# First head pair of a clustered attention: tokens paired in a transpose, loads of 1536 bytes, one head's chain at a time

## The chip, the core and the metric

One core of a Trainium2 chip runs the whole program. TensorE (PE) does matmuls and transposes, and PEld is its weight load; VectorE is DVE, ScalarE is ACT, GpSimd is POOL, and SP (SyncE) issues most transfers. The metric is the time of one execution on the device, in microseconds. The median of three runs of the kernel before is 1048.67 us (1047.87 to 1049.45).

## The reference, cut to what matters

Attention in which a query sees only the keys of its own cluster comes first; two mixtures of experts follow, and the change does not touch them.

```python
B, H, S, D = 2, 8, 768, 64          # 16 clusters per head
q_n, k_n, c_n = (x / (norm(x) + 1e-6) for x in (q, k, centroids))
q_assign = argmax(einsum('bhsd,hcd->bhsc', q_n, c_n), -1)
k_assign = argmax(einsum('bhsd,hcd->bhsc', k_n, c_n), -1)
mask   = q_assign[..., :, None] == k_assign[..., None, :]
scores = where(mask, q @ k.T / sqrt(D), -1e9)
attn   = softmax(scores)
x      = attn @ v                    # then two expert mixtures
```

## The kernel before, in words

Two heads make a pair and there are eight pairs. An item is one tile of 128 queries of one head against its 768 keys, so a pair has 12 items, and the attention 96 (`attention`, L618). Each fp32 operand is split into a rounded part `hi` and a remainder `lo`, and products are taken as hi·hi + lo·hi + hi·lo.

For an item PE makes the scores `S` (`scores`, L490: two matmuls of 128 rows, two of 80; L504), DVE takes their maximum `nm` (L507), ACT the exponential `P` (`expo`, L510), PE turns `P` round in six transposes (`ptrans`, L518), ACT copies the result out as `ph` (L527) and DVE makes the remainder `pl` (L528). From item 4 on PE also multiplies by the values (`pv`, L530). The scores run two items ahead (AHEAD = 2). The first step of the loop therefore makes the scores of item 2, and it takes the PSUM buffer that item 0's exponential must have read: there are two `S` buffers.

Before its scores a pair needs a preparation (`prep`, L197). Its q and k are loaded with 128 tokens on the partitions and both heads' 64 dimensions side by side, so each token gives a run of 256 bytes for a head. `turn` (L278) transposes three tiles of 128x128, `copies` (L289) makes `hi` on ACT, `low` (L302) makes `lo`. `sims` (L318) multiplies by the normalised centroids, `product` (L340) turns that back to tokens, and the steps `a0` to `a6` of `arg_first` (L382) take the argmax on DVE and write it as one-hot rows 64 to 79 of the operands `L2` and `R2`. For the first pair this is done head by head, `a00` to `a60` for the first and `a01` to `a51` and `onehot` for the second; a same-cluster score is shifted up by a large number through these 16 rows, which is the mask. `rows0` and `rows1` (L439) copy `hi` and `lo` by SBUF transfers of 192 KB into `L1, L2, R1, R2` of the two heads.

To begin before these transfers land, items 0 and 1 take the three products straight from `hi` and `lo` with 64 rows (`products`, L479, steps `O 0` and `O 1`; six matmuls each, L486), and only the 16 mask rows are added later (`S 0`, `S 1`, two matmuls each). `E 0` and `E 1` are their exponentials.

The order is written by hand. `START` lists the steps ahead of the loop; each step issues its instructions on every engine's queue in that order, and every engine runs its queue in order. `W 24` is 24 matmuls of no use, which keep PE running while the loads are on their way. The steps with a `1` in front prepare the second pair. `FIRST` places the rest in the loop by (item, position): position 0 is behind the item's scores, 1 ahead of its transposes, 2 at its end. SP's queue has the transfers in the same order. PSUM tiles of tag `T` go round three buffers; tag `PV` has one, used by the transposes `k0`, `k1`, `q0` of the second pair (L281) as well as by `pv`. In the second pair `copies` makes two ACT copies of each transpose, and POOL subtracts them (L306).

Of the kernel before, what the change touches and what calls it, by code (L numbers as in the profile page):

```python
# [5 lines left out]
F32 = mybir.dt.float32  # L6
F32R = mybir.dt.float32r
# [21 lines left out]
def r2(ap):  # L29
    return ap.rearrange("p (a b) -> p a b", a=2)  # L30

# [51 lines left out]
class Net:  # L83
# [13 lines left out]
    def consts(self):  # L97
# [9 lines left out]
        self.cb = c.tile([128, 4, 160], F32R, name="cb")  # L107
        nc.gpsimd.memset(self.cb.bitcast(F32), 0.0)
# [26 lines left out]
    def centroids(self, p):  # L135
# [4 lines left out]
        xx = p.tile([128, 2 * D], F32, name="cxx", bufs=1)  # L140

        def scale():
            r = self.cr
            nc.vector.tensor_scalar(r, r, 1e-6, None, op0=ALU.add)
            nc.vector.reciprocal(r, r)
            nc.vector.tensor_scalar(xx[:, 0:D], x, r, None, op0=ALU.mult)
            nc.vector.tensor_scalar(xx[:, D:2 * D], x, r, None, op0=ALU.mult)

        def place():
            ps = self.ps.tile([128, 128], F32, name="cT", tag="T", bufs=3)  # L150
            nc.tensor.transpose(ps, xx, self.ident)
            ch = p.tile([128, 128], F32R, name="ch")
            cl = p.tile([128, 128], F32R, name="cl")
            nc.scalar.activation(ch, ps, AF.Copy)
            nc.vector.tensor_tensor(cl, ps, ch.bitcast(F32), op=ALU.subtract)
            for hh in range(2):
                rows = slice(hh * 64, hh * 64 + 64)
                for part, src in ((0, ch), (1, cl)):
                    sv = src[rows].bitcast(F32).rearrange("p (a h c) -> p a h c", a=4, h=2)[:, :, hh, :]
                    o = 32 + part * 64 + hh * 16  # L160
                    nc.gpsimd.tensor_copy(self.cb[rows, :, o:o + 16], sv)
# [9 lines left out]
        return norm, scale, place  # L171
# [25 lines left out]
    def prep(self, n):  # L197
# [4 lines left out]
        first = n == 0  # L202
# [12 lines left out]
        def square(s, m, hh=None):  # L215
            def go():
# [4 lines left out]
                if hh is not None:  # L221
                    nc.scalar.activation(P["sq"][:, s, :, hh], x[m][:, :, hh * 64:hh * 64 + 64], AF.Square)
                    return
# [6 lines left out]

        def total(s, hh):
            nc.vector.tensor_reduce(P["sqs"][:, s, :, hh], P["sq"][:, s, :, hh], axis=AX.X, op=ALU.add)

        def power(s, hh):
            o = self.rn2[0][:, hh * 2 * NT:hh * 2 * NT + 2 * NT, 0].rearrange("p (t s) -> p t s", s=2)
            nc.gpsimd.tensor_tensor(o[:, :, s], P["sqs"][:, s][:, :, hh], self.half[:, 0:NT], op=ALU.pow)
# [14 lines left out]
        def vsplit(hh):  # L251
            def go():

                if hh == 0:
                    P["vv"] = self.vvp.tile([128, NT, 4, 64], F32R, name="vv", tag="vv")
                hi, lo = P["vv"][:, :, 3 * hh, :], P["vv"][:, :, 1 + hh, :]
                xv = x["v"][:, :, hh * 64:hh * 64 + 64]
                if ON["vhi"] == "act":
                    nc.scalar.activation(hi, xv, AF.Copy)
                else:  # L260
                    nc.vector.tensor_copy(hi, xv)
                nc.gpsimd.tensor_tensor(lo, xv, hi.bitcast(F32), op=ALU.subtract)
            return go

        scales = {"q": 0.125, "k": 1.0}
# [74 lines left out]
        def product():  # L340
            sn = P["sn"] = self.ps.tile([128, NT, 64], F32, name="sn", tag="T", bufs=3)
# [3 lines left out]
        def arg1():  # L345
            product()
            sn = P["sn"]
# [992 lines left out]
```

## Time and profile before

| | us |
|---|---|
| median of three runs | 1048.67 |
| the profiled execution, its own time | 1048.17 |
| its span in the profile | 1046.1 |
| TensorE's mean granted clock (share of full) | 0.997 |

The profiled execution lies 0.5 us below the median, and its span 2.07 us below its own time, which is what lies around the span. Starts are us from the start of the span. In a timeline row come start, duration, engine, line, operation, out<-in, shapes, count, and in brackets the idle time ahead and what ended it. Merged rows cover several instructions.

### The profile page before, as it was taken

What the parts mean: (1) busy time and instruction counts of PE and PEld (TensorE: products, weight loads), DVE (VectorE), ACT (ScalarE), POOL (GpSimd) and SP (SyncE); (2) the same over time, 40 slices, a digit from 0 to 9 for tenths busy, and PEclk for the clock granted to TensorE, in tenths of its full rate; (3) what the DMA queues carried; (4) which work ended last, traced back from release to release, by engine and by line L of the source; (5) the groups of instructions that cost most, each with busy time, mean ns of one, the idle gap of its engine ahead of it and who ended that gap; (6) DMA issues with size and microseconds to landing.
All of it is one profiled execution on the core that took longest, in us unless ns stands there. A gap on an engine that the chain in (4) does not pass through costs nothing.

```text
span 1046.1 us, 16203 instructions
## 1 busy us (share of the span) xinstructions
PE 1031.5 (99%) x5795; PEld 962.8 (92%) x5795; DVE 812.5 (78%) x1414; ACT 544.0 (52%) x1150; POOL 631.1 (60%) x577
## 2 busy tenths in 40 slices
PE   8999999999999999999999999999999999999998
PEld 6999999998999999999999899899889989989987
DVE  7899999998887777777787876776777876676675
ACT  5989989889654444444354333333353333333320
POOL 6676677988676868666768444444444644444430
PEclk8999999999999999999999999999999999999999
DMA  9668977663122222122212221221213221221201
GB/s 197 154 153 191 207 163 179 141 161 101 51 69 72 61 81 61 62 61 65 78 40 81 81 81 41 81 81 41 81 61 122 81 81 46 76 81 59 63 21 60
DMA packets 86543, 95.94 MB, mean 92 GB/s; under 512 B 42752, under 2 KB 59488, under 8 KB 86464
## 3 DMA queue, kind: packets, MB, share of 16 engines
q1 hardware_dynamic: 86320, 94.89, 33.5%
q8 instruction: 45, 0.74, 0.3%
q14 instruction: 34, 0.28, 0.1%
q10 hardware_dynamic: 144, 0.03, 0.0%
HBM read 65.07 MB, written 3.19 MB: 65 GB/s over the span
## 4 chain that ended last, share of the span: by engine, by line
PE 84%; DVE 5%; POOL 4%; ACT 3%; DMA 2%; issue 2%; SPq 0%; DVEq 0%; POOLq 0%; ACTq 0%
PE ph L886 34%; PE po L1207 8%; PE po L1208 8%; PE po L1206 8%; PE po L985 7%; PE S L504 5%; PE T L524 4%; PE PV L537 2%; PE PV L538 2%; DMA L<-loq 1%; PE T L286 1%; PE sn L343 1%; PE sT L325 1%; DVE ph L921 1%; DVE pl L528 1%
## 5 line engine op out<-in xcount | busy, mean ns | idle before, releaser
L1162 POOL TENSOR_TENSOR wol<-r,woh 128x512 fp32r<-128x512 f32 x62 | 80.0, 1292 | 152.2 <-ACT woh L1161 152.1
L1213 DVE SCALAR_TENSOR_TENSOR acc<-po,pn,acc 128x512 f32<-128x512 f32 (+1 forms) x181 | 129.8, 742 | 36.3 <-PE po L1208 36.3
L1208 PE MATMUL po<-woh,h2l 128*128 128x512 f32 (+1 forms) x374 | 145.7, 389 | 0.0
L1207 PE MATMUL po<-wol,h2h 128*128 128x512 f32 (+1 forms) x374 | 145.6, 389 | 0.0
L1206 PE MATMUL po<-woh,h2h 128*128 128x512 f32 (+1 forms) x374 | 145.0, 388 | 0.0
L804 POOL TENSOR_TENSOR w1l<-sf,w1h 128x512 fp32r<-128x512 f32 x88 | 115.2, 1329 | 43.5 <-ACT w1h L801 43.3
L1181 ACT ACTIVATE h2h<-ph 128x384 fp32r<-128x384 f32 x128 | 62.4, 490 | 119.4 <-PE ph L886 93.3
L886 PE MATMUL ph<-h,w1h 128*128 128x384 f32 x336 | 114.0, 339 | 1.6 <-ACT sg L958 1.0
L886 PE MATMUL ph<-h,w1l 128*128 128x384 f32 x336 | 112.7, 336 | 0.0
L886 PE MATMUL ph<-l,w1h 128*128 128x384 f32 x336 | 112.6, 335 | 0.0
L528 DVE TENSOR_TENSOR pl<-T,ph 128x384 fp32r<-128x384 f32 x192 | 97.5, 549 | 18.2 <-ACT ph L527 17.1
L985 PE MATMUL po<-G,woh 128*128 128x384 f32 x384 | 101.7, 338 | 1.2 <-DVE acc L997 0.3
L801 ACT ACTIVATE w1h<-sf 128x512 fp32r<-128x512 f32 x86 | 54.4, 632 | 83.3 <-DVE sf L792 68.7
L1182 DVE SCALAR_TENSOR_TENSOR h2l<-ph,h2h 128x384 fp32r<-128x384 f32 x128 | 71.0, 554 | 34.3 <-ACT h2h L1181 31.2
L504 PE MATMUL S<-R,L 80*128 80x384 f32 (+2 forms) x380 | 91.3, 362 | 2.4 <-ACT P L515 1.4
L507 DVE TENSOR_REDUCE nm<-S 128x1 f32<-128x768 f32 x96 | 91.1, 949 | 1.5 <-PE S L504 0.6
L527 ACT ACTIVATE ph<-T 128x384 fp32r<-128x384 f32 x192 | 84.2, 494 | 14.2 <-PE T L524 14.1
L804 POOL TENSOR_TENSOR w1l<-r,w1h 128x512 fp32r<-128x512 f32 x64 | 67.6, 1056 | 37.4 <-ACT w1h L801 37.4
L515 ACT ACTIVATE P<-S,nm 128x768 f32<-128x768 f32 x96 | 87.6, 913 | 0.7 <-DVE nm L507 0.5
L524 PE MATMUL T<-ident,P 128*128 128x128 f32 x576 | 82.0, 276 | 2.1 <-DVE pl L528 1.6
L1208 PEld LDWEIGHTS po<-woh,h2l 128*128 128x128 f32 x374 | 70.2, 188 | 14.5
L1207 PEld LDWEIGHTS po<-wol,h2h 128*128 128x128 f32 x374 | 70.2, 188 | 13.9
(309 smaller groups left out, 2759.4 us busy)
## 6 DMA issues: line engine op xcount, KB each, us to landing
r<-in_moe_w_dram SPq DMA_DIRECT2D x64, 512.0 KB, 3.8
raw<-in_moe_w_val_dram SPq DMA_DIRECT2D x12, 512.0 KB, 3.8
L<-hiq SPq DMA_DIRECT2D x28, 192.0 KB, 4.8
R<-hik SPq DMA_DIRECT2D x28, 192.0 KB, 4.2
rwo<-in_moe_w_out_dram SPq DMA_DIRECT2D x10, 512.0 KB, 3.5
raw<-in_moe_w_gate_dram SPq DMA_DIRECT2D x10, 512.0 KB, 3.9
nv<-in_v_dram SPq DMA_DIRECT2D x16, 192.0 KB, 3.7
A<-U SPq DMA_DIRECT2D x16, 192.0 KB, 3.7
```

What stands on the lines that cost most here:

```text
L504: nc.tensor.matmul(ps[:, a, 0:384], l[k, c], r[k, a * 384:a * 384 + 384], start=l is L1, stop=l is L2)
L507: nc.vector.tensor_reduce(nm, ps[:, :, 0:384], axis=AX.XY, op=ALU.max, negate=True)
L515: nc.scalar.activation(r2(pt), ps[:, :, 0:384], AF.Exp, bias=nm, scale=1.0, accum_out=P["sums"][:, i, 0:1])
L524: nc.tensor.transpose(ps[:, j, :], pt[:, c:c + 128], self.ident)
L528: nc.vector.tensor_tensor(lo, ps, hi.bitcast(F32), op=ALU.subtract)
L804: nc.gpsimd.tensor_tensor(lo[:, sl], x, hi[:, sl].bitcast(F32), op=ALU.subtract)
L886: nc.tensor.matmul(ps, x[:, a, j], y[:, j], start=first and j == 0 and k == 0, stop=j == 1 and k == 2, skip_group_check=not first)
L985: nc.tensor.matmul(ps, t[x][:, dc], y[:, f, c], start=f == 0 and k == 0, stop=f == 1 and k == 2)
L1206: nc.tensor.matmul(ps, Hh[:, f, c], wh[:, dc], start=f == 0, stop=False)
L1207: nc.tensor.matmul(ps, Hh[:, f, c], wl[:, dc], start=False, stop=False)
L1208: nc.tensor.matmul(ps, Hl[:, f, c], wh[:, dc], start=False, stop=f == 1)
L1213: nc.vector.scalar_tensor_tensor(a, ps, pe, a, op0=ALU.mult, op1=ALU.add)
```

## The change

It replaces the first pair's preparation by `prep_first`. Six consecutive tokens of a head lie on one partition, so a load moves runs of 1536 bytes and a head is a transfer of its own, in the order q and k of the first head, then of the second. One 128x128 transpose turns two tokens (r = 0, 1) with 64 dimensions each, so three transposes hold all 768 tokens of one head, in two halves of rows. The second half of the keys must be moved to the first 64 partitions (`near`, two transfers of 96 KB) before items 0 and 1 can use it: their three products come in two steps, `O` and `Z`. Item 2 also takes the three products, in place of the 128-row and 80-row matmuls. `rows0` to `rest1` move halves, 96 KB each. In the second pair the four ACT copies for POOL go, and `low` reads PSUM on DVE for all four (`on = "dve"`). The centroids get a second placement for the first pair (`cb0`), and `spread` fills the old one later. `L` numbers below are those of before.

```diff
 START = [
-    "W 24", "0 sq_q0", "0 sum_q0", "0 pow_q0", "0 scale", "1 load_q", "0 q0", "0 q1", "W 5", "0 place", "0 sq_k0", "1 load_k",
-    "W 3", "0 sum_k0", "0 pow_k0", "0 k0", "0 k1", "0 rows0", "0 sq_q1", "0 sq_k1", "0 sims0", "0 sims1",
-    "0 sum_q1", "0 sum_k1", "0 pow_q1", "0 pow_k1", "0 a00", "0 product", "1 sq_q", "O 0", "0 a10", "1 turn_k0", "1 copy_k0",
-    "O 1", "1 turn_k1", "1 copy_k1", "0 a20", "0 a30", "0 a40", "0 a50", "1 low_k0", "1 low_k1",
-    "0 rows1", "0 load_v", "0 a01", "0 a11", "0 a60", "1 sq_k", "S 0", "1 turn_q0", "1 copy_q0", "1 fold1", "1 fold2", "1 low_q0",
-    "S 1", "0 a21", "E 0", "E 1", "0 a31",
+    "W 26", "1 load_q", "0 sq_q0", "0 turn_q0", "W 3", "0 copy_q0", "0 scale", "0 sum_q0", "0 pow_q0", "0 place", "0 low_q0", "W 3",
+    "0 turn_k0", "0 sq_k0", "0 copy_k0", "0 sum_k0", "0 pow_k0", "0 low_k0", "0 near", "1 load_k", "0 rows0",
+    "0 mq0", "0 turn_q1", "0 mk0", "0 sq_q1", "0 copy_q1", "0 st0", "0 sum_q1", "0 pow_q1", "0 low_q1", "0 product0",
+    "0 a00", "O 0", "0 turn_k1", "O 1", "0 sq_k1", "0 copy_k1", "0 a10", "0 a20", "0 a30", "0 a40", "0 a50",
+    "0 spread", "0 low_k1", "0 sum_k1", "0 pow_k1", "1 sq_q", "Z 0", "Z 1", "0 a60", "0 mq1", "0 load_v", "0 rows1",
+    "1 sq_k", "S 0", "0 mk1", "0 st1", "S 1", "0 a70", "0 product1", "1 fold1", "1 fold2",
+    "0 a01", "0 a11", "E 0", "0 a21", "E 1",
 ]
 FIRST = {
-    "1 turn_q1": (0, 0), "1 copy_q1": (0, 0), "1 low_q1": (0, 0), "0 a41": (0, 1), "0 a51": (0, 2), "1 root": (0, 2),
-    "1 sims0": (1, 0), "0 onehot": (1, 2), "0 mask1": (1, 2), "0 v0": (1, 2), "1 sims1": (2, 0), "1 rows0": (2, 1),
-    "1 rows1": (4, 1), "1 arg0": (3, 2), "1 arg1": (3, 2), "0 v1": (4, 0), "1 arg2": (4, 1), "1 arg3": (4, 2),
+    "2 load_q": (1, 2), "2 load_k": (1, 2), "1 turn_k0": (0, 0), "1 copy_k0": (0, 0), "1 low_k0": (0, 0), "0 a31": (0, 0), "0 a41": (0, 1), "0 a51": (0, 2),
+    "1 turn_k1": (0, 2), "1 copy_k1": (0, 2), "1 low_k1": (0, 2), "1 root": (0, 2), "0 onehot": (1, 0), "0 mask1": (1, 0),
+    "0 rest1": (1, 1), "1 turn_q0": (1, 0), "1 copy_q0": (1, 0), "1 low_q0": (1, 0), "0 v0": (1, 2),
+    "1 turn_q1": (2, 0), "1 copy_q1": (2, 0), "1 low_q1": (2, 0), "1 sims0": (2, 2), "1 sims1": (3, 0), "1 rows0": (3, 1),
+    "1 arg0": (3, 2), "1 arg1": (3, 2), "0 v1": (4, 0), "1 arg2": (4, 1), "1 rows1": (5, 0), "1 arg3": (4, 2),
...
         def copies(m, a):
...
-                on = "dve" if first else "mix" if n == 1 else ON[m + str(a)]
+                on = "dve" if n == 1 else ON[m + str(a)]
...
+        for hh in range(2):
+            for m, src in (("q", self.q), ("k", self.k)):
+                if hh == 0:
+                    x[m] = self.nat0.tile([128, 2, S // 2], F32, name="n" + m, tag="n" + m)
+                dma(out=x[m][:, hh], in_=src[b, pr * 2 + hh].rearrange("(p t) d -> p (t d)", t=NT))
...
+        def turn_(m, hh):
+            o = ps[m, hh] = self.ps.tile([128, 384], F32, name="T", tag="T", bufs=3)
+            for a in range(3):
+                c = slice(a * 128, a * 128 + 128)
+                nc.tensor.transpose(o[:, c], x[m][:, hh, c], self.ident)
...
+        def sim_(m, hh):
...
+            for part in range(2):
+                nc.tensor.matmul(sT[hh], self.cb0[:, hh, 32 - s * 32:160 - s * 32], hl[m][part][:, hh * 384:hh * 384 + 384],
+                                 start=s + part == 0, stop=s + part == 2)
...
+        def product(hh):
+            o = sn[hh] = self.ps.tile([128, 3, 64], F32, name="sn", tag="T", bufs=3)
+            for a in range(3):
+                c = hh * 384 + a * 128
+                nc.tensor.matmul(o[:, a], P["sTs"][:, c:c + 128], self.stk, start=True, stop=True)
...
+        keys = [("R1", 0, "kh"), ("R2", 0, "kl"), ("R1", 64, "kh")]
+        queries = [("L1", 0, "qh"), ("L1", 64, "ql"), ("L2", 0, "qh")]
+        def near():
+            rows(0, [k + (1,) for k in keys[:2]])
+        def rows0():
+            rows(0, [keys[2] + (1,)] + [k + (0,) for k in keys] + [q + (1,) for q in queries])
+        def rows1():
+            rows(1, [k + (r,) for k in keys for r in range(2)] + [q + (0,) for q in queries])
+        def rest1():
+            rows(1, [q + (1,) for q in queries])
...
+    def products(self, t, halves, ps=None):
...
+        for a in halves:
+            for i, (x, y) in enumerate(((0, 0), (1, 0), (0, 1))):
+                self.nc.tensor.matmul(ps[:, a, 0:384], hl["q"][x][0:64, t * 128:t * 128 + 128],
+                                      R[y][0:64, 384:S] if a else hl["k"][y][0:64, 0:384], start=i == 0, stop=False)
...
-            begin["O %d" % i] = lambda i=i: sc.update({i: self.products(i)})
+            begin["O %d" % i] = lambda i=i: sc.update({i: self.products(i, (0,))})
+            begin["Z %d" % i] = lambda i=i: self.products(i, (1,), sc[i])
...
-            sci = self.scores(*items[i + AHEAD]) if i + AHEAD < len(items) else None
+            sci = self.scores(*items[i + AHEAD], *([self.products(2, (0, 1))] if i == 0 else [])) \
+                if i + AHEAD < len(items) else None
```

`sq`, `sum`, `pow`, `copy`, `low`, `m` and `st` of the new list are the old square, sum, root, `hi` copy, `lo`, `sims` matmuls and their copy, each for one operand and one head. `a60` writes one-hot rows of the first 384 queries, `a70` those of the others.

## Rows read from the trace of the kernel before

**Rows 1.** The page: busy time by engine, and the chain that ended last by engine.

```profile
PE 1031.5 (99%) x5795; PEld 962.8 (92%) x5795; DVE 812.5 (78%) x1414; ACT 544.0 (52%) x1150; POOL 631.1 (60%) x577
...
PE 84%; DVE 5%; POOL 4%; ACT 3%; DMA 2%; issue 2%; SPq 0%; DVEq 0%; POOLq 0%; ACTq 0%
```

**Rows 2.** Stretches: window, PE, PEld, DVE, ACT, POOL busy; granted clock; DMA share; GB/s.

```profile
16.00:18.00 2.00, 0.98 (x14) 0.74 (x11) 1.01 (x2) 1.95 (x4) 1.10 (x2) 1.00 1.00 212
18.00:20.00 2.00, 1.29 (x7) 0.60 (x5) 1.63 (x2) 1.62 (x4) 1.46 (x1) 0.86 0.94 199
20.00:22.00 2.00, 1.35 (x4) 1.35 (x5) 1.86 (x4) 1.48 (x4) 1.84 (x3) 0.50 0.89 201
...
26.00:28.00 2.00, 2.00 (x17) 1.70 (x16) 0.94 (x2) 1.36 (x4) 2.00 (x1) 0.93 0.00 1
```

**Rows 3.** The chain of waits to 60 us, pieces in order: start, duration, what.

```profile
5.20 1.51 PE T L286 x6
...
12.39 1.24 PE S L486 x6
...
20.65 1.65 PE S L504 x4
...
25.50 1.12 PE sT L325 x4
...
31.99 1.47 PE sn L343 x12
...
49.35 0.71 PE sT L325 x4
50.06 0.66 PE T L524 x6
50.72 0.70 PE S L504 x4
```

**Rows 4.** Timeline of ACT, 3 to 22 us.

```profile
4.05 0.52 ACT L222 ACTIVATE sq<-nq 128x384 f32<-128x384 f32 x1 [1.83 <-DMA nq<-in_q_dram]
6.11 0.49 ACT L299 ACTIVATE hiq<-T 128x384 fp32r<-128x384 f32 x1 [1.53 <-PE T L286]
...
16.80 0.80 ACT L431 ACTIVATE R<-oT 16x768 fp32r<-16x768 bf16 x1
...
19.60 0.91 ACT L515 ACTIVATE P<-S,nm 128x768 f32<-128x768 f32 x1
```

**Rows 5.** Timeline of DVE, 3 to 32 us.

```profile
8.21 0.55 DVE L232 TENSOR_REDUCE sqs<-sq 128x6 f32<-128x384 f32 x1
8.97 1.20 DVE L308 SCALAR_TENSOR_TENSOR lok<-T,hik 128x384 fp32r<-128x384 f32 x2 [0.21 <-ACT hik L299]
...
12.43 0.36 DVE L399 TENSOR_TENSOR sim<-sn,rh 128x192 f32<-128x192 f32 x1 [0.99 <-PE sn L343]
...
14.38 0.36 DVE L420 TENSOR_TENSOR oh<-w,code 128x192 bf16<-128x192 f32 x1
...
18.30 1.98 DVE L507 TENSOR_REDUCE nm<-S 128x1 f32<-128x768 f32 x2 [0.62 <-PE S L504]
...
20.65 0.99 DVE L409 TENSOR_TENSOR w<-sim,mx 128x192 f32<-128x192 f32 x1
...
27.55 1.02 DVE L528 TENSOR_TENSOR pl<-T,ph 128x384 fp32r<-128x384 f32 x2 [1.06 <-ACT ph L527]
```

**Rows 6.** Timeline of PE, 12 to 36 us.

```profile
15.80 0.84 PE L429 MATMUL oT<-identb,oh 128*16 128x128 bf16 x12
17.65 0.61 PE L504 MATMUL S<-R,L 16*128 16x384 f32 x2 [1.02 <-ACT R L431]
...
33.27 0.95 PE L504 MATMUL S<-R,L 128*128 128x384 f32 x4
```

**Rows 7.** SBUF copies of L448 to 40 us: issue, ns min/median/max; landing, us.

```profile
L448 SPq DMA_DIRECT2D R<-hik x4: 462/805/982, 9.6 to 12.9; - x4
...
DMA to landing us min/median/max: 3.2/4.0/4.2
```

More of the change, by code (lines that the diff above doesn't have):

```diff
@@ L30, in r2, with r3 @@
     return ap.rearrange("p (a b) -> p a b", a=2)
+def r3(ap):
+    return ap.rearrange("p (a b) -> p a b", a=3)
 SLOT = {
@@ L145, in scale, with parts, spread @@
             nc.vector.reciprocal(r, r)
-            nc.vector.tensor_scalar(xx[:, 0:D], x, r, None, op0=ALU.mult)
-            nc.vector.tensor_scalar(xx[:, D:2 * D], x, r, None, op0=ALU.mult)
+            nc.vector.tensor_scalar(xx[:, 0:4:3], x.unsqueeze(1).to_broadcast([128, 2, D]), r, None, op0=ALU.mult)
+        def parts(o, v):
+            nc.scalar.activation(o(0), v, AF.Copy)
+            nc.vector.tensor_tensor(o(1), v, o(0).bitcast(F32), op=ALU.subtract)
         def place():
[L150 to L155, printed above, removed]
-            for hh in range(2):
[L157 to L161, printed above, removed]
+            ps = T["ps"] = self.ps.tile([128, 2, 128], F32, name="PV", tag="PV", bufs=1)
+            for r in range(2):
+                nc.tensor.transpose(ps[:, r], xx[:, 2 * r:2 * r + 2].rearrange("p a d -> p (a d)"), self.ident)
+            parts(lambda part: self.cb0[:, :, 32 + part * 64:64 + part * 64].rearrange("p h (r c) -> p h r c", r=2),
+                  ps[:, :, 0:32].rearrange("p r (h c) -> p h r c", h=2))
+        def spread():
+            for hh in range(2):
+                parts(lambda part: self.cb[:, :, 32 + part * 64 + hh * 16:48 + part * 64 + hh * 16],
+                      T["ps"][:, hh].rearrange("p (a h c) -> p a h c", a=4, h=2)[:, :, hh])
         def norm():
@@ L169, in norm @@
             nc.gpsimd.tensor_tensor(r, sq, self.half[:, 0:1], op=ALU.pow)
-        return norm, scale, place
+        return norm, scale, place, spread
     def probs(self):
@@ L201, in prep @@
         P = self.pairs[n] = {}
-        first = n == 0
         x, hl = {}, {}
@@ L229, in square @@
             return go
[L231 to L236, printed above, removed]
         def fold(ws):
@@ L443, in go @@
                 qh, ql, kh, kl = (t.bitcast(F32)[hh * 64:hh * 64 + 64] for t in hl["q"] + hl["k"])
-                order = (1, 2, 0, 4, 5, 3) if hh else (0, 4, 3, 1, 2, 5) if first else range(6)
+                order = (1, 2, 0, 4, 5, 3) if hh else range(6)
                 parts = [(L1[0:64], qh), (R1[0:64], kh), (R1[64:128], kh), (L1[64:128], ql), (L2[0:64], qh),
@@ L456, in mask @@
             return go
-        if first:
-            for go in (load("q", self.q), load("k", self.k)):
-                go()
-            return [("load_v", load("v", self.v)), ("q0", qkt("q", 0)), ("q1", qkt("q", 1)), ("scale", self.cscale), ("place", self.cplace),
-                    ("k0", qkt("k", 0)), ("k1", qkt("k", 1)), ("rows0", rows(0)), ("rows1", rows(1)),
-                    ("sims0", sims(0)), ("sims1", sims(1)), ("product", product)] + \
-                [("%s_%s%d" % (w, m, hh), go) for s, m in ((0, "q"), (1, "k")) for hh in range(2)
-                 for w, go in (("sq", square(s, m, hh)), ("sum", lambda s=s, hh=hh: total(s, hh)),
-                               ("pow", lambda s=s, hh=hh: power(s, hh)))] + arg_first(0) + arg_first(1) + \
-                [("onehot", onehot), ("mask1", mask(1)), ("v0", vsplit(0)), ("v1", vsplit(1))]
         sums = [("fold1", fold((32,))), ("fold2", fold((16, 8, 4, 2, 1)))]
@@ L476, in prep @@
             ("arg2", arg2), ("arg3", arg3), ("rows1", rows(1)), ("arg4", arg4), ("arg5", arg5),
-            ("onehot", onehot), ("mask0", mask(0)), ("mask1", mask(1)), ("v0", vsplit(0)), ("v1", vsplit(1)))]
-    def products(self, t):
-        hl = self.pairs[0]["hl"]
-        ps = self.psS.tile([128, 2, 512], F32, name="S", tag="S")
-        c = slice(t * 128, t * 128 + 128)
-        for i, (x, y) in enumerate(((0, 0), (1, 0), (0, 1))):
-            for a in range(2):
-                self.nc.tensor.matmul(ps[:, a, 0:384], hl["q"][x][0:64, c], hl["k"][y][0:64, a * 384:a * 384 + 384],
-                                      start=i == 0, stop=False)
+            ("onehot", onehot), ("mask0", mask(0)), ("mask1", mask(1)),
@@ new lines, in prep, with vsplit @@
+            ("v0", lambda: self.vsplit(P, x, 0)), ("v1", lambda: self.vsplit(P, x, 1)))]
+    def vsplit(self, P, x, hh):
+        nc = self.nc
+        if hh == 0:
+            P["vv"] = self.vvp.tile([128, NT, 4, 64], F32R, name="vv", tag="vv")
+        hi, lo = P["vv"][:, :, 3 * hh, :], P["vv"][:, :, 1 + hh, :]
+        xv = x["v"][:, :, hh * 64:hh * 64 + 64]
+        if ON["vhi"] == "act":
+            nc.scalar.activation(hi, xv, AF.Copy)
+        else:
+            nc.vector.tensor_copy(hi, xv)
+        nc.gpsimd.tensor_tensor(lo, xv, hi.bitcast(F32), op=ALU.subtract)
@@ L1283, in run @@
                 self.consts()
-                cnorm, self.cscale, self.cplace = self.centroids(self.pm)
-                self.prep0 = self.prep(0)
+                self.scales = {"q": 0.125, "k": 1.0}
+                cnorm, self.cscale, self.cplace, self.cspread = self.centroids(self.pm)
+                self.prep0 = self.prep_first()
                 cnorm()
```

205 lines of the change are left out of this document (136 added, 69 removed).

## The prediction

> **What bounds the kernel now.** I read the page first: PE is busy 99% of the span and makes up 84% of the chain that ended last [rows 1]. From item 6 on the loop is the same in both kernels and PE runs it without a gap, so a change to the beginning is worth what it shifts the start of item 6's scores, at 33.27 us [rows 6]. I call this start the mark. The only room lies ahead of it. The stretches show where [rows 2]: from 16 to 22 us PE is busy 0.98, 1.29 and 1.35 us in each 2 us, and the granted clock goes from 1.00 (2.4 GHz) over 0.86 to 0.50 (1.2 GHz); it is back in the stretch from 26 us. The chain of waits then shows what PE waited for: it goes through the first exponentials on ACT, from 19.60, before PE makes item 2's scores at 20.65 [rows 3, 4]. The timelines of ACT, DVE and PE give the steps ahead of that: the first head's q arrives at 4.05 but the transposes wait until 5.20 for the second head's [rows 3, 4]; the argmax runs from 12.43 to 14.74, its transposes at 15.80, ACT's one-hot rows at 16.80, the mask matmuls at 17.65, the maxima from 18.30 to 20.28, the first exponential at 19.60 [rows 4 to 6].
>
> **Part 1, up to the first exponential.** `turn_q0` needs one head only and can start at 4.0, when the 26 warm matmuls are about done. The copy follows 0.91 later, as in 5.20 to 6.11 [rows 3, 4]. Behind it PE has three warm matmuls, two centroid transposes, three more and `turn_k0`: at the 0.25 of a transpose here (1.51 for six [rows 3]) about 1.85, so `turn_k0` at 5.85 and `copy_k0` at 6.76 to 7.25. DVE is then in `low_q0` (0.60) and `sum_k0` (0.55 [rows 5]); `low_k0` runs 7.40 to 8.00. Then `mk0`, 0.65 until its result can be read (17.65 to 18.30 [rows 5, 6]), `st0` 0.49: 9.2. `product0` is half of 1.47 [rows 3]: 10.0. The six argmax steps take 2.31 as before, so the one-hots are there at 12.35, against 14.74: 2.4 earlier.
>
> PE is not free then. `O 0`, `turn_k1`, `O 1`, `Z 0`, `Z 1` stand ahead of `a60` in its queue; two times 1.24 and a transpose step of 0.4 from 9.95 make 12.85, so 0.5 is lost. `Z` also needs the `near` copies, the second of which leaves SP at 8.03 behind `low_k0`. Copies land 3.2 to 4.2 after issue [rows 7]: 11.2 to 12.2, with `Z 0` due at 11.6. These carry half the bytes and stand behind two loads fewer, so I take 0, and keep 0 to 0.6 late. Whatever `Z` waits, `a60` and everything behind it wait. From 12.85: half of the 0.84 of transposes and 0.2 to release ACT, 0.80 for the rows, so `S 0` at 14.3; the maximum 0.65 later, 0.99 long [rows 5]: `E 0` at 16.0 against 19.60, **3.6 earlier**.
>
> The wider transfers give nothing on this path beyond that: k of the first head comes by 5.1 if each takes the 1.0 of before and its transpose is due at 5.85; if they are faster it waits as long. Bounds: 0 to 0.3 for the first load. SP issues 11 transfers more, in halves. Eleven issues of 0.8 [rows 7] stand from `near` (7.3) to the end of `rows0`, so it has left by 16.1, lands by 20.3 at the longest, and is needed at 21.5 by item 3; `rows1` and the mask follow in SP's queue and are needed only at the mark. The cover is 1 us; without it, item 3 is late by the rest. The pow steps on POOL and the second head's squares lie beside this chain. The new memsets come in POOL's idle time ahead of the centroids: 0.
>
> **Part 2, from the first exponential to the mark.** Item 2 waits for the buffer of item 0: 16.0 + 0.91 + 0.14 (20.65 less 20.51 [rows 3, 4]) is 17.05. Its six 64-row products take 1.24, the mask matmuls 0.65 until DVE can read: the maximum starts at 18.95. Here the change puts its own load: four `low` of the second pair, formerly on POOL and half of them ahead of the loop, now stand in DVE's queue. Up to the last of them DVE has three maxima (2.97), four argmax steps (1.56 at a pitch of 0.39), four `low` (2.40) and four `pl` (2.04): 8.97 [rows 5], and it is at 27.9. PE can't go round it: `turn_k1` and `turn_q0` need the one PV buffer that `low_k0` and `low_k1` free, and `sims0` needs the T buffer that `low_q1` frees. So PE mostly waits between 19.6 and 23.5 and again ahead of 27.9. Behind that PE alone decides: `sims0` 0.71, item 5's scores 0.70, `sims1` 0.71, six transposes 0.66, the product 1.47 [rows 3]: 4.25, and the mark is at **32.15 against 33.27, 1.1 earlier**. What ACT loses (four copies of 0.39) is no part of the sum, since it waits for DVE in this stretch.
>
> So of 3.6 won, 2.5 is given back: item 2 costs 0.9 more on PE, and the rest is the second pair's preparation, which before filled PE's and ACT's waits ahead of the loop and now stands in it. One row weighs on the sum: DVE's two-input step at 20.65 took 0.99 instead of 0.36, beside POOL's additions [rows 5]. These additions now run some 3 us earlier, beside `a11`, where DVE waits for item 2 anyway: 0, bounds 0 to 0.6.
>
> The rows show 0.207 for a 64-row matmul (1.24 for six) against 0.175 for one of 128 rows [rows 3]. The Trainium skill (TensorE: Matmul & The Clock Gate, Why this matters for your kernels) says of a matmul of few rows that it takes the "same time as K=128". By that item 2 would be read 0.2 sooner and the mark be 1.3 earlier; the row decides here, and the sum keeps 0.207.
>
> **The sum.** The profiled execution took 1048.17, 0.5 below the median: 1048.17 - 1.1 + 0.5 = 1047.55, taken as 1047.5. A measurement of this kernel can tell about 0.2% (2.1 us) from no change; the forecast lies within.
>
> **Rivals.**
> - *The lead is kept.* If DVE's steps overlap at their ends or the T ring lets PE do half of its 4.25 beneath DVE's stretch, 2.1 more stays: 3.2 earlier, 1045.5, faster. For it: PE's own work from 17.05 to the mark is only 10.5 (item 2 1.6, four preparations at 0.33, four times 0.66, three times 0.70, twice 0.71, 1.47) of 15.1. Against: the single PV buffer.
> - *The clock falls on the new wait, once, and DVE's room covers most.* Between 19.6 and 23.5 PE has 1.3 us of work (item 3's scores, one preparation, the one-hots), a third, less than the half to two thirds of the stretches ahead of the old fall [rows 2]. Transposes and scores that feed DVE come late by about 1 us: 1048.5, the same.
> - *The clock is still low when PE decides.* Place: the 4.25 behind 27.9. At 1.2 GHz a `sims` took 1.12 for 0.71, scores 1.65 for 0.70 [rows 3], so 2.5 to 5.9 more; with 3.4, 2.3 later than before: 1051.0, slower. It decides once over 3.2 is lost there. Against: before, two stretches with nearly full PE brought the clock back. The Trainium skill (the same page, HAM oscillation) tells of kernels whose matmuls come in bursts between waits and which drop to the low clock again at each wait; by that rule this case would come, and the rows of before, with one fall in the beginning, bear it out only in part.
> - *The change doesn't do what it says:* head 0's chain is not sooner, because both loads or `near` land late. Each us that `near` is late takes one from 3.6; above 1.1 nothing is left and the time is 1048.7.
>
> **How the numbers follow.** Forecast 0.37; one fall or late copies, about no change, 0.19; the lead kept 0.31; the low clock on PE's tail 0.13. Faster is the 0.31 and 0.02 of the forecast's own spread: 0.33. Slower is 0.13, same 0.54. The range leaves out the far halves of the outer cases: 1045.1 to 1050.2.
>
> **What would show it.** In the profile of the changed kernel: one-hots of the first head at 12.4 and `E 0` near 16.0 (part 1); item 2's scores over 1.5 us long; DVE without a gap from about 19 to 28; PE idle behind item 0's transposes and ahead of `sims0`; item 6's scores at 32.1. Wrong would be a mark at 30 or earlier (PE passed DVE), `Z 0` waiting for a DMA beyond 12, or a granted clock of 0.50 beyond 28.

## The result and the profile after

The changed kernel took 1053.65 us (median of six runs, 1052.48 to 1055.32) against 1048.27 for the kernel before, measured beside it (six runs, 1046.85 to 1049.45): a ratio of 1.0054, 95% interval 1.004 to 1.0068. It is slower, by 5.4 us; the forecast was 1047.5. Runs of one kernel can lie some us apart here (1046.2 to 1055.0 in d_no_warm below), so ranges stand beside the medians. The profiled execution took 1054.22 with a span of 1052.4, against 1048.17 and 1046.1 before. Item 6's scores, the mark, start at 39.59 instead of 33.27 [rows 6]: 6.32 later, and the span is 6.3 longer. From the mark to the end both take 1012.8, so in sum all of the loss lies ahead of the mark.

The page, busy time and the chain that ended last, by engine, as in [rows 1]:

```profile
PE 1038.8 (99%) x5797; PEld 967.8 (92%) x5797; DVE 813.7 (77%) x1420; ACT 542.6 (52%) x1148; POOL 626.9 (60%) x571
...
PE 87%; DVE 4%; POOL 4%; ACT 2%; issue 2%; DMA 1%; SPq 0%; DVEq 0%; POOLq 0%; ACTq 0%
```

PE is busy 7.3 us longer with two matmuls more: the same work takes longer. ACT and POOL have less to do (1.4 and 4.2 us), DVE 1.2 us more, and PE's share of the chain rises from 84% to 87%. The stretches, as in [rows 2]:

```profile
16.00:18.00 2.00, 2.00 (x15) 1.44 (x13) 0.00 (x0) 1.28 (x2) 1.32 (x1) 1.00 0.77 177
18.00:20.00 2.00, 2.00 (x7) 1.03 (x5) 0.61 (x2) 1.20 (x2) 0.70 (x1) 1.00 0.94 210
20.00:22.00 2.00, 2.00 (x6) 1.12 (x5) 1.01 (x2) 0.99 (x2) 1.92 (x2) 1.00 0.68 158
```

The holes of before are gone, PE is busy without a gap, and DVE does 1.6 us of work in these 6 where it did 4.5. The granted clock reads 1.00, which would be 2.4 GHz. The timeline of PE says otherwise:

```profile
9.98 1.54 PE L483 MATMUL sn<-stk,sTs 128*128 128x64 f32 x6 [0.58 <-ACT sTs L477]
...
15.95 0.52 PE L598 MATMUL S<-R,loq 64*128 64x384 f32 x1
16.27 0.52 PE L598 MATMUL S<-R,hiq 64*128 64x384 f32 x1
16.72 1.45 PE L554 MATMUL oT<-identb,oh 128*16 128x128 bf16 x12
...
19.03 1.01 PE L616 MATMUL S<-R,L 16*128 16x384 f32 x2
...
27.16 1.49 PE L636 MATMUL T<-ident,P 128*128 128x128 f32 x6
...
31.46 0.82 PE L636 MATMUL T<-ident,P 128*128 128x128 f32 x6
...
39.59 0.94 PE L616 MATMUL S<-R,L 128*128 128x384 f32 x4
...
55.62 0.59 PE L616 MATMUL S<-R,L 80*128 80x384 f32 x2 [1.09 <-DMA R<-ohT]
```

Two matmuls of 384 columns start 0.32 us apart (15.95, 16.27), which is 384 columns at 1.2 GHz. The twelve transposes of the one-hots take 1.45, against 0.84 before [rows 6], and six transposes of `P` 1.49 at 27.16 but 0.82 at 31.46. So the clock was low until about 30.6, and the column doesn't show it: the trace's first record of the clock is the rise at 30.56, and ahead of its first record the column reads 1.00. This is the profiled execution. The mean granted clock of the six runs was 0.999 (this one), 0.992, 0.991, 0.995, 0.994 and 1.0; in the four below 0.999 a longer low stretch is on record, so the clock had risen sooner and fallen again, as in the profiles of a_dma and d_sq_alone below (both 0.991); they were nearly as late (1052.48 to 1054.32). The last row is a wait that before has not: PE stands 1.09 us for the mask rows of the second pair. It hardly shows at the end: matched matmul by matmul and counted from the mark, the changed kernel is 1.4 behind d_no_warm (below) after it and 0.4 at the end. ACT, as in [rows 4], and DVE, as in [rows 5]:

```profile
3.26 0.52 ACT L438 ACTIVATE sq<-nq 128x384 f32<-128x384 f32 x1 [1.04 <-DMA nq<-in_q_dram]
...
16.03 0.84 ACT L235 ACTIVATE sq<-R 128x768 f32<-128x768 f32 x1 [1.26 <-DVE sqs L442]
17.56 0.80 ACT L555 ACTIVATE R<-oT 16x768 fp32r<-16x768 bf16 x1 [0.69 <-PE oT L554]
...
21.40 0.89 ACT L627 ACTIVATE P<-S,nm 128x768 f32<-128x768 f32 x1
```

```profile
1.39 1.98 DVE L121 CAST identb<-ident 128x128 bf16<-128x128 f32 x1 [0.36 <-POOL ident masks.py:199]
...
3.69 0.23 DVE L178 TENSOR_TENSOR csx<-cx 128x64 f32<-128x64 f32 x1
...
13.51 0.36 DVE L541 TENSOR_TENSOR oh<-w,code 128x192 bf16<-128x192 f32 x1
...
26.57 0.96 DVE L619 TENSOR_REDUCE nm<-S 128x1 f32<-128x768 f32 x1 [1.76 <-PE S L616]
...
34.62 0.56 DVE L296 SCALAR_TENSOR_TENSOR hl<-T,hl 128x384 fp32r<-128x384 f32 x1
```

The first load arrives at 3.26 instead of 4.05 [rows 4], and the one-hots are there at 13.87, 0.87 sooner than before [rows 5]. Then the lead goes: the first exponential starts at 21.40, 1.80 later than before [rows 4]. DVE waits 1.76 for item 2's scores.

### The profile page after: what moved, and what is told of

Read it like the earlier page. It is cut to its first block, busy times and chain, and to the rows that moved or that the text cites. A ratio compares the mean times of both kernels' runs of the same rounds, so it can differ in the third digit from the quotient of the medians.

```text
span 1052.4 us, 16224 instructions
## 1 busy us (share of the span) xinstructions
PE 1038.8 (99%) x5797; PEld 967.8 (92%) x5797; DVE 813.7 (77%) x1420; ACT 542.6 (52%) x1148; POOL 626.9 (60%) x571
## 4 chain that ended last, share of the span: by engine, by line
PE 87%; DVE 4%; POOL 4%; ACT 2%; issue 2%; DMA 1%; SPq 0%; DVEq 0%; POOLq 0%; ACTq 0%
PE ph L1003 35%; PE po L1324 8%; PE po L1325 8%; PE po L1323 8%; PE po L1102 8%; PE S L616 5%; PE T L636 5%; PE PV L649 3%; PE PV L650 3%; PE sn L331 1%; PE sT L313 1%; PE S L598 1%; DVE ph L1038 1%; POOL w1l L921 1%; PE T L274 1%
## 5 line engine op out<-in xcount | busy, mean ns | idle before, releaser
L616 PE MATMUL S<-R,L 128*128 128x384 f32 (+2 forms) x378 | 91.6, 363 | 1.1 <-DMA R<-ohT 1.1
L639 ACT ACTIVATE ph<-T 128x384 fp32r<-128x384 f32 x192 | 84.0, 494 | 14.7 <-PE T L636 14.3
L1323 PEld LDWEIGHTS po<-woh,h2h 128*128 128x128 f32 x374 | 70.2, 188 | 13.9
```

Of the source, the lines that this page charges most:

```text
L616: nc.tensor.matmul(ps[:, a, 0:384], l[k, c], r[k, a * 384:a * 384 + 384], start=l is L1, stop=l is L2)
L639: nc.scalar.activation(hi, ps, AF.Copy)
L1323: nc.tensor.matmul(ps, Hh[:, f, c], wh[:, dc], start=f == 0, stop=False)
```

## Experiments

Two theories stood at first. **Clock:** the beginning is lost because PE runs it at 1.2 GHz. **Order:** it is lost because of where the work now stands (remainders in DVE's queue, row copies later). The table gives each kernel's excess over the median of before, measured beside it; that of the change is +5.4.

| run | median (range), us | ratio, 95% interval | excess |
|---|---|---|---|
| a_warm | 1052.03 (1050.31–1052.91) | 1.0032, 1.002–1.0044 | +3.8 |
| a_rows128 | 1051.24 (1049.89–1054.48) | 1.0035, 1.0022–1.0048 | +3.0 |
| a_dma | 1051.59 (1049.63–1053.78) | 1.0031, 1.0019–1.0043 | +3.3 |
| b_few_warm | 1048.33 (1046.15–1053.06) | 1.0006, 0.9992–1.0019 | +0.1 |
| c_warm_dma | 1050.18 (1048.98–1051.07) | 1.0019, 1.0011–1.0028 | +2.2 |
| c_rows128 | 1049.78 (1048.79–1051.52) | 1.0017, 1.0007–1.0026 | +1.8 |
| c_mix | 1053.16 (1051.65–1054.26) | 1.0049, 1.0034–1.0063 | +5.2 |
| c_sq | 1046.35 (1045.55–1048.26) | 0.9988, 0.9979–0.9996 | -1.6 |
| d_sq_alone | 1049.13 (1047.24–1053.28) | 1.0025, 1.0011–1.004 | +1.8 |
| d_no_warm | 1051.79 (1046.22–1054.98) | 1.0038, 1.0021–1.0056 | +4.5 |
| d_memset | 1047.76 (1045.74–1048.74) | 0.9999, 0.9988–1.0009 | +0.5 |
| d_item2 | 1051.91 (1051.01–1053.68) | 1.0046, 1.0034–1.0059 | +4.6 |

**a_warm: thirteen more matmuls of no use in PE's waits.**

```diff
-    "W 26", "1 load_q", "0 sq_q0", "0 turn_q0", "W 3", "0 copy_q0",
+    "W 26", "1 load_q", "0 sq_q0", "0 turn_q0", "W 10", "0 copy_q0",
...
-    "0 mq0", "0 turn_q1", "0 mk0", "0 sq_q1",
+    "0 mq0", "0 turn_q1", "0 mk0", "W 6", "0 sq_q1",
```

> After, with ten warm matmuls in place of three behind the first transposes and six more ahead of the first head's product, so that TensorE has no gap up to item 0's products. Theory clock (the 25 us in which TensorE runs at 1.2 GHz, up to 30.8 us, are what made the change slower): matmuls are at the 2.4 GHz pitch by about 10 us, E 0 comes at 17 us instead of 21.4, item 6's scores at 33 to 35 instead of 39.6, the time falls by 4 to 6 us to about 1048.5. Rival order (the second pair's preparation in DVE's queue and the single buffer set the pace): item 6's scores move by less than 1 us, and so does the time.

The clock was high from about 4.7, as far as the pitch of PE's matmuls tells. ACT's timeline, and below it PE's:

```profile
14.02 0.84 ACT L235 ACTIVATE sq<-R 128x768 f32<-128x768 f32 x1 [1.26 <-DMA R<-hik]
14.88 0.80 ACT L555 ACTIVATE R<-oT 16x768 fp32r<-16x768 bf16 x1
...
17.44 0.90 ACT L627 ACTIVATE P<-S,nm 128x768 f32<-128x768 f32 x1
```

```profile
12.91 0.84 PE L554 MATMUL oT<-identb,oh 128*16 128x128 bf16 x12
...
15.74 0.61 PE L616 MATMUL S<-R,L 16*128 16x384 f32 x2 [1.44 <-ACT R L555]
...
34.79 0.95 PE L616 MATMUL S<-R,L 128*128 128x384 f32 x4
```

The first exponential came at 17.44 instead of 21.40 and the mark at 34.79 instead of 39.59, both where the clock theory wants them. The median fell by only 1.6, below the theory's 4 to 6. In the profiled execution 2.1 of the 4.8 won at the mark is lost behind it: 1014.9 from the mark to the end against 1012.8, with a wait of 1.1 in the expert mixtures (at 310 us) that the changed kernel's profile has not. The rows also show a wait that nobody had priced: the one-hot rows (L555) stand behind `1 sq_q`, the second pair's squares (L235), which take their single buffer (tag `sq`, one buffer) only when DVE has summed the first pair's last squares (13.39 to 13.93 here). The row names a DMA as what ended the wait; in the changed kernel the same wait is put down to DVE's sum (16.03, above). PE waits 1.44 for the one-hot rows, and later the granted clock falls (0.59 in the stretch from 18 to 20).

**a_rows128: the 64-row products take all 128 rows.** Within the clock theory the few rows of these matmuls may be what keeps the clock low, or the kind of matmul has no part in it.

```diff
-    ps[:, a, 0:384], hl["q"][x][0:64, t * 128:t * 128 + 128],
-    R[y][0:64, 384:S] if a else hl["k"][y][0:64, 0:384],
+    ps[:, a, 0:384], hl["q"][x][:, t * 128:t * 128 + 128],
+    hl["k"][y][:, 0:384],
```

> After, where the early products of items 0 to 2 use all 128 rows of the operands and the same keys for both halves, as many matmuls as before; the scores of these three items are so another sum (both tokens of a pair are added up). Theory kind of work (the clock stayed low although TensorE had no gap from 10 us on, because 64-row and 16-row matmuls filled this time): the clock rises between 13 and 20 us instead of 30.8, the time falls by 3 to 5 us. Rival (the kind of matmul has no part in it): half speed up to about 30 us as before, time within 0.7 us of 1053.6.

The profiled execution was at the low clock until about 10, then high until 16.6. The median is 2.4 lower, but runs of the 64-row kernel differ in their clock too (above), and this edit also takes away the wait of the second halves for the `near` copies; c_rows128 repeats it where the clock is high from about 7.

**a_dma: the second pair's row copies where they were before, and the third pair's loads ahead of them.**

```diff
-    "2 load_q": (1, 2), "2 load_k": (1, 2), "1 rows0": (3, 1), "1 rows1": (5, 0),
+    "2 load_q": (0, 2), "2 load_k": (0, 2), "1 rows0": (2, 1), "1 rows1": (4, 1),
```

> After, with the loads of the third pair put back ahead of the mask copies and the second pair's row copies one step earlier, as before the change. Theory (the late row and mask copies of the second pair cost the 1.1 us wait at 55 us, apart from the clock): this wait goes, time 1.0 to 1.5 us lower. Rival (another engine would hold TensorE there anyway): the same within 0.5 us.

The stretches of this kernel:

```profile
10.00:12.00 2.00, 2.00 (x10) 1.58 (x10) 1.78 (x5) 0.60 (x2) 0.29 (x1) 0.83 0.94 227
...
16.00:18.00 2.00, 2.00 (x6) 1.07 (x5) 0.74 (x2) 0.70 (x1) 1.22 (x1) 0.50 0.90 218
...
50.00:60.00 10.00, 10.00 (x69) 9.79 (x68) 9.08 (x17) 9.82 (x24) 5.80 (x7) 1.00 0.81 192
```

PE is busy in all of 50 to 60, against 8.91 in the changed kernel, and the wait of 1.09 is gone. The median is 2.0 lower, but that is not the price of the copies: in the profiled execution the mark comes at 37.21, 2.38 sooner, because the clock was high from about 4.5 to 11.3, and from the mark to the end it takes 1012.6 against 1012.8. What the earlier copies are worth by themselves is not shown; the wait that goes is 1.09. The other two rows show the clock on record: it fell at 11.3 and stayed at 0.50 until 28.4 although the profile has PE busy throughout.

**b_few_warm: the kernel before, without its own `W 5` and `W 3`.**

```diff
-    "0 q0", "0 q1", "W 5", "0 place", "0 sq_k0", "1 load_k",
-    "W 3", "0 sum_k0",
+    "0 q0", "0 q1", "0 place", "0 sq_k0", "1 load_k",
+    "0 sum_k0",
```

> Before, without the five and the three warm matmuls ahead of the first key transposes. Theory clock: before was fast because TensorE's clock rose at 9 us, behind a stretch without a gap; with gaps the clock rises later, the beginning runs at 1.2 GHz for 3 to 10 us longer, and the time grows by 1.5 to 5 us. Rival (the low clock in the beginning is hidden by other engines): within 0.7 us of 1048.3.

No difference in the median, but two runs of twelve took 1053.04 and 1053.06, above every run of before. One of them was profiled: low clock until about 31, and the mark at 38.39, near the changed kernel's 39.59. The old order too loses 5 us when its clock doesn't rise; none of the 24 runs of before measured beside it (up to 1050.16) shows that. Two of twelve against none of 24 may be chance.

**c_warm_dma and c_rows128: both edits together, and with them the 128 rows.** The diffs are those of a_warm and a_dma, and for c_rows128 also of a_rows128.

> After with both edits of the first experiments together: the 13 warm matmuls more and the third pair's loads and second pair's row copies put back. Theory (two separate losses, the low clock and the late row copies): the gains add up, 1.6 and 2.1 off 1053.65, about 1050; no wait for the mask copies at 50 to 56 us. Rival (they overlap): not below 1051.3.

> The same, with 128 rows in the early products of items 0 to 2 (their scores are another sum, as in the earlier run with 128 rows). Theory kind of work (few-row matmuls keep the clock from rising again and help it to fall): the low stretch is shorter, time 1 to 2.5 us below the kernel with 64 rows. Rival: within 0.7 us of it, with the same low stretch.

The median gains add up nearly: 1.6 and 2.0 alone, 3.2 together, and the wait at 55 us is gone. With 128 rows 0.4 more, inside both intervals. That the 64 rows hold the clock down is not supported.

**c_mix: the second pair's remainders back on POOL in halves.**

```diff
-                on = "dve" if n == 1 else ON[m + str(a)]
+                on = "mix" if n == 1 else ON[m + str(a)]
```

> The same as the first of this call, with the second pair's remainders back on POOL and its two copies on ACT, as before the change. Theory order (the four remainders in DVE's queue hold up the one PV buffer, and with it TensorE): the transposes of the second pair no longer wait for DVE, item 6's scores come 1 to 1.5 us sooner and the time falls by about 1 us. Rival (ACT's four copies more and POOL's 1.0 us per remainder cost as much as DVE's queue): within 0.7 us, or slower.

It is 3.0 slower than c_warm_dma. PE's timeline shows the wait:

```profile
32.71 0.94 PE L313 MATMUL sT<-hl,cb 128*128 128x384 f32 x4 [1.85 <-POOL hl L294]
```

In c_warm_dma PE waits 1.03 at this place. The remainders on DVE are not the loss; from POOL they come later still. The order theory falls in this point.

**c_sq: c_warm_dma, with `1 sq_q` behind the one-hot rows** (and two of the new memsets behind the sixteen constants on POOL, which left DVE's `csx` at 3.68).

```diff
-    "0 pow_k1", "1 sq_q", "Z 0", "Z 1", "0 a60", "0 mq1", "0 load_v", "0 rows1",
-    "1 sq_k", "S 0",
+    "0 pow_k1", "Z 0", "Z 1", "0 a60", "0 mq1", "0 load_v", "0 rows1",
+    "1 sq_q", "1 sq_k", "S 0",
```

> The first of this call, with the second pair's square of q behind the first head's one-hot rows on ACT instead of ahead of them, and the two new memsets behind the other constants on POOL. Theory (ACT's rows wait for that square, which waits for the square buffer until DVE's sum at 13.9 us; TensorE then has a gap from 14 to 15.7 us): E 0 at 16.0 to 16.3 instead of 17.4, a shorter low clock, time 1.2 to 3 us below the first of this call. Rival (the DVE stretch behind E 0 gives the lead back): less than 0.5 us.

ACT's timeline of this kernel:

```profile
13.70 0.80 ACT L555 ACTIVATE R<-oT 16x768 fp32r<-16x768 bf16 x1 [0.70 <-PE oT L554]
14.52 1.58 ACT L235 ACTIVATE sq<-R 128x768 f32<-128x768 f32 x2
16.37 0.89 ACT L627 ACTIVATE P<-S,nm 128x768 f32<-128x768 f32 x1
```

The mark, in PE's timeline:

```profile
33.80 0.95 PE L616 MATMUL S<-R,L 128*128 128x384 f32 x4
```

The one-hot rows are 1.18 sooner than in a_warm, the first exponential 1.07 and the mark 0.99, with low stretches of the clock that are equally long (6.8 us in both). At 1046.35 this is faster than both kernels, by 1.6 than before, with an interval that ends at 0.9996. Its profiled execution (1048.21) was one of its later ones and still had a fall of the clock from 17.0 to 23.9, with the mark at 33.80; 7 of 11 runs were at or below 1046.4.

**d_sq_alone: the changed kernel with only the move of `1 sq_q`** (the diff of c_sq, memsets as in the change).

> After, with one edit alone: the second pair's square of q behind the first head's one-hot rows on ACT. Theory square (this place in ACT's queue is the largest single loss, whatever the clock does): 1050 to 1051, 2.5 to 3.8 below 1053.65. Rival (with the gaps in TensorE's first 10 us and the low clock that follows, TensorE is later than ACT at this place, and the square costs nothing): above 1052.5.

The median is 3.6 lower against before, 3.0 by the ratios, but it is the last of a lower group: six of eleven runs took 1047.24 to 1049.13, the other five 1052.24 to 1053.28, where the changed kernel is. One of the five was profiled; its clock was low from 12.9 to 29.9. From PE and ACT of this kernel, and below them the same steps in a_dma, where the squares stand ahead and the clock was low too:

```profile
14.48 1.45 PE L554 MATMUL oT<-identb,oh 128*16 128x128 bf16 x12
19.16 0.90 ACT L627 ACTIVATE P<-S,nm 128x768 f32<-128x768 f32 x1
```

```profile
14.19 1.45 PE L554 MATMUL oT<-identb,oh 128*16 128x128 bf16 x12
18.88 0.90 ACT L627 ACTIVATE P<-S,nm 128x768 f32<-128x768 f32 x1
```

From the transposes to the first exponential it is 4.68 with the move and 4.69 without it (4.68 in the changed kernel): at the low clock the place of the squares costs nothing, as the rival says. At the high clock it is 4.53 without the move (a_warm) and 3.22 with it (d_no_warm, below), so there it is worth 1.3. The 3.0 to 3.6 is therefore no price of this wait; it depends on how many runs had the clock high. Why more of them did here is not shown.

**d_no_warm: c_sq without the thirteen matmuls of a_warm.** Its diff is that of a_warm, turned round.

> The best kernel so far (1046.35) without its 13 additional warm matmuls. Theory clock (gaps in the first 10 us leave the clock low for longer): 1.5 to 3 slower, 1048 to 1049.5, and more spread from run to run. Rival (the square's place was all): within 0.7 us of 1046.35.

The median is 5.4 above that of c_sq, more than the theory's 3. One kernel gave three levels: 1046.22 to 1046.79 (three runs), 1051.36 to 1052.34 (five), 1053.42 to 1054.98 (four). The profiled execution is the fastest run, and its clock was high from about 5.7, without the extra matmuls. It is the nearest test of the forecast, since the order is that of the change but for `1 sq_q`, the two memsets and later transfers. PE, DVE and ACT:

```profile
12.46 0.34 PE L598 MATMUL S<-R,loq 64*128 64x384 f32 x1
12.64 0.34 PE L598 MATMUL S<-R,hiq 64*128 64x384 f32 x1
12.90 0.84 PE L554 MATMUL oT<-identb,oh 128*16 128x128 bf16 x12
...
14.38 0.58 PE L616 MATMUL S<-R,L 16*128 16x384 f32 x2
...
32.00 0.94 PE L616 MATMUL S<-R,L 128*128 128x384 f32 x4
```

```profile
11.99 0.36 DVE L541 TENSOR_TENSOR oh<-w,code 128x192 bf16<-128x192 f32 x1
...
19.04 0.96 DVE L619 TENSOR_REDUCE nm<-S 128x1 f32<-128x768 f32 x1
...
27.06 0.56 DVE L296 SCALAR_TENSOR_TENSOR hl<-T,hl 128x384 fp32r<-128x384 f32 x1
```

```profile
16.12 0.89 ACT L627 ACTIVATE P<-S,nm 128x768 f32<-128x768 f32 x1
```

The transposes start at 12.90, the first exponential at 16.12, DVE's last remainder ends at 27.62 and the mark is at 32.00: the forecast had 12.85, 16.0, 27.9 and 32.15. Against the changed kernel's profile the mark is 7.6 sooner. The granted clock fell once more here (0.75 in the stretch from 18 to 20, 0.50 from 20 to 22, 1.00 again from 24), which the forecast doesn't have; DVE's last remainder is not later for it.

**d_memset: c_sq with the zeros written by DVE and POOL's constants put off.**

```diff
-        nc.gpsimd.memset(self.cb.bitcast(F32), 0.0)
+        nc.vector.memset(self.cb.bitcast(F32), 0.0)
...
-        nc.gpsimd.memset(self.cxx, 0.0)
-        nc.gpsimd.memset(self.cb0.bitcast(F32), 0.0)
+        nc.vector.memset(self.cb0.bitcast(F32), 0.0)
+        nc.vector.memset(self.cxx, 0.0)
```

> The best kernel so far with the zeros of the centroid tiles written by DVE and the 16 small constants behind the centroids' root, so that POOL writes less while DVE makes its two first copies. Theory (DVE's copies of the identity end only when POOL's memsets end: 2.8 us before the change, 3.37 after): the centroid sum starts at 2.9 to 3.2 instead of 3.68, E 0 comes 0.4 to 0.6 earlier, time 0.3 to 0.7 lower. Rival (DVE's own memsets take what is won, or the first head's chain does not hang on the centroids): within 0.3 us.

DVE's timeline:

```profile
2.23 0.16 DVE L121 CAST identb<-ident 128x128 bf16<-128x128 f32 x1
...
3.35 0.23 DVE L176 TENSOR_TENSOR csx<-cx 128x64 f32<-128x64 f32 x1 [0.54 <-DMA cx<-in_centroids_dram]
```

ACT's:

```profile
15.66 0.89 ACT L625 ACTIVATE P<-S,nm 128x768 f32<-128x768 f32 x1
```

The identity copy takes 0.16 instead of 1.98, and the centroids' squares start 0.33 sooner, now held by their load. The first exponential comes 0.71 sooner than in c_sq and 0.46 sooner than in d_no_warm, as the theory says. The time doesn't show it: the median lies 1.4 above c_sq's, and the runs fall into the same two groups as there (five up to 1046.35, seven from 1047.76). In the profiled execution the clock was low for 10.2 us (17.5 to 27.7) against 6.8 in c_sq, and the mark, at 33.48, is 0.32 sooner all the same; what the memsets cost at the mark is not shown.

**d_item2: c_sq with ordinary scores for item 2**, so with three more row copies ahead and the second pair's k behind them.

```diff
-    "0 near", "1 load_k", "0 rows0",
+    "0 near", "0 rows0", "1 load_k",
...
-    rows(0, [keys[2] + (1,)] + [k + (0,) for k in keys] + [q + (1,) for q in queries])
+    rows(0, [keys[2] + (1,)] + [k + (0,) for k in keys] + [q + (r,) for q in queries for r in range(2)])
...
-    sci = self.scores(*items[i + AHEAD], *([self.products(2, (0, 1))] if i == 0 else [])) \
+    sci = self.scores(*items[i + AHEAD], *[]) \
```

> The best kernel so far with item 2's scores made by two 128-row and two 80-row matmuls, as before the change; for this three more row copies go ahead and the second pair's load of k stands behind them. Theory (item 2's eight matmuls cost 0.8 us more than four at the high clock and 1.6 to 1.9 at the low one, on the chain): item 2's maximum starts 0.8 to 1.9 earlier and the time is 0.5 to 1.5 lower. Rival (the row copies land later than item 0's exponential ends, at 17.3 us, or the late load holds the second pair up): the same or slower.

ACT's timeline:

```profile
20.00 0.84 ACT L235 ACTIVATE sq<-R 128x768 f32<-128x768 f32 x1 [4.68 <-DMA R<-in_k_dram]
...
21.12 0.89 ACT L627 ACTIVATE P<-S,nm 128x768 f32<-128x768 f32 x1
```

The second pair's k lands 4.7 us too late for the squares in ACT's queue, and the first exponential waits behind them. Item 2 from 64 rows is cheaper than that.

## Why the prediction was wrong

The chain that it named was right but for one wait, and so was the room on each engine; **the durations of PE in part 1 were taken at the wrong clock**, and the wait of `1 sq_q` was left out. Its terms against the two profiled executions (start in us unless said):

| step | forecast | changed kernel | d_no_warm |
|---|---|---|---|
| `turn_q0` | 4.0 | 3.84 | 3.83 |
| `turn_k0` | 5.85 | 6.45 | 6.08 |
| one-hots done | 12.35 | 13.87 | 12.35 |
| transposes of `a60` | 12.85 | 16.72 | 12.90 |
| `S 0` | 14.3 | 19.03 | 14.38 |
| `E 0` | 16.0 | 21.40 | 16.12 |
| maximum of item 2 | 18.95 | 26.57 | 19.04 |
| end of the last `low` | 27.9 | 35.18 | 27.62 |
| mark | 32.15 | 39.59 | 32.00 |

- *Part 1 failed.* "Two times 1.24 and a transpose step of 0.4", "half of 1.47" and "the 0.84 of transposes" are durations at 2.4 GHz. At the clock that was there, a product of 384 columns costs 0.32 instead of the 0.207 taken, six matmuls of `product0` 1.54 instead of 0.73, twelve transposes 1.45. From `product0` to the transposes of `a60` PE has no gap in either profile: 6.74 in the changed kernel (9.98 to 16.72), 3.78 in d_no_warm (9.12 to 12.90), 3.65 in the forecast. So 0.8 late at `product0` is 3.9 late at the transposes and 5.4 at `E 0`. The rows held the sign: six transposes took 1.51 at 5.20 and 0.66 at 50.06 [rows 3], so before too began at the low clock. The sum took 0.25 for a transpose up to `turn_k0` and the short durations for what follows, and never asked when the clock would rise.
- *Item 2 failed for the same reason.* From `E 0` to its maximum the forecast has 2.95, the changed kernel 5.17, d_no_warm 2.92.
- *Part 2 held from there.* From item 2's maximum to the end of the last `low` it gave 8.97; 8.61 and 8.58 were measured. PE's tail to the mark was given 4.25; 4.41 and 4.38 were measured. DVE gives up what was won at `E 0`, as said.
- *The wait of `1 sq_q` was missed.* In the changed kernel it costs nothing visible (its squares end at 16.87, the transposes at 18.17), but as soon as the clock is high it holds the one-hot rows, as a_warm shows: with the clock high up to 18.4 the order of the change gives `E 0` at 17.44 instead of 16.0, and the mark at 34.79, still behind the 33.27 of before. So the forecast would have failed at its own clock too, by this wait (1.0 at the mark, a_warm against c_sq) and by the fall of the clock behind it. The single buffer of the squares ties the second pair's first step to the first pair's last.
- *The row copies behind the mark were not priced.* "From item 6 on the loop is the same" overlooked that `FIRST` also moves `1 rows0`, `1 rows1` and the loads, and that their mask rows then come late: 1.09 of waiting at 55.62, of which 0.4 is left at the end of the profiled execution (against d_no_warm).
- *The near copies, the 1536-byte runs and `rows0`* were rightly costed at nothing: PE has no gap from 10 to 18, nor in d_no_warm from 9.9 to 13.7, where `Z 0` starts at 11.76 without a wait. The first load is 0.8 sooner, where 0 to 0.3 was allowed. *The memsets* were put at 0 and cost 0.56 on the centroids' chain (`csx` at 3.69 against 3.13): PE waits 0.67 for the centroids ahead of `turn_k0`, which is about the 0.60 that this step is late in the table.
- *The rivals.* The one on the other side put the low clock on PE's tail, as a fall after a wait; here it was low from the start and gone by 30.6, before the tail, which kept its 4.41. (By its own rows the upper bound is 5.8, not 5.9.) That it too ends slower than before is luck. The Trainium skill (TensorE: Matmul & The Clock Gate, HAM oscillation) ties the low clock to waits between bursts. That describes a_warm, where the clock falls after the wait of 1.44, but not the changed kernel's 10 to 18 us, in which the profile shows PE busy for 8.00 of 8.00. The page's other rule, that few rows take the same time as 128, is borne out for the pitch: about 0.175 between two 64-row matmuls in d_no_warm (0.18 from 12.46 to 12.64). The sum was right to keep 1.24 all the same: item 2's six took 1.25 there up to the mask matmuls (17.15 to 18.40), since the first of them and the change at the end take longer.

Shown by runs: with `1 sq_q` moved and the clock high from 5.7 to about 19 PE gives the forecast's times within 0.3 (d_no_warm; in part luck, since a fall of the clock and the wait for the centroids are in it too); the move of `1 sq_q` is worth 1.3 at `E 0` at the high clock and nothing at the low one. The changed kernel's mark is 7.6 behind that of d_no_warm, and the profiled executions between them give the steps, one each and with the other edits in them: 4.8 with a clock high until 18.4 (a_warm), 1.0 with the move (c_sq), 1.8 with a shorter fall of the clock (d_no_warm). Not shown: why the clock rises at 5 us in one run and at 30 in another. With the 13 matmuls no run of c_sq was above 1048.3, without them nine of twelve of d_no_warm were above 1051, but neither rows (c_rows128) nor the place of the remainders (c_mix) explained the rest.

## What to carry to other kernels

Before taking a duration from a row for work that is moved to the first 30 us, ask at which clock the row ran and whether PE will run at that clock in the new order; then price the queue once at either level. The chain of small matmuls on PE's path took 6.74 at the low level and 3.78 at the high one, so here the early rise was worth more than the shorter chain. And where a step of the next pair is moved ahead of a step of this one, look for the buffer that both share.

## What the runs showed of the hardware

- A profile's granted clock can read 1.00 where matmuls run at 1.2 GHz: 1.00 over 0 to 30 us in the changed kernel while 384 columns took 0.32 us. The pitch of equal matmuls decides; the prediction's sign "a granted clock of 0.50 beyond 28" would have missed this. The Trainium skill (TensorE: Matmul & The Clock Gate, Seeing it yourself) calls the recorded events unreliable on trn2; here the recorded ones agree with the pitch (the rise at 30.56, a_dma's fall at 11.3), and what misleads is the 1.00 ahead of the first.
- The low clock held for 17 us (a_dma, 11.3 to 28.4) with PE shown busy throughout.
- One kernel has several times: 1046.2, about 1052 and about 1054 in d_no_warm, with a mean granted clock of 0.998, 0.990 to 0.992 and 0.999 to 1.0. These are the means of its own profile, of a_dma's (0.991) and of the changed kernel's (0.999); the later levels were not profiled.
- DVE's copy of a 128x128 identity took 1.98 us while POOL wrote its memsets, and ended 0.09 after the last of them (3.28); with DVE writing the zeros itself it took 0.16.
